# First half of the k weights on ScalarE's DMA queue in two loads, x tile 3 between the row blocks of the second half

## Chip, cores, metric

The kernel runs on one core of a Trainium2 chip. The metric is the device time of one execution in microseconds; the time before is the median of three runs.

## What is computed

The input x has 2048 rows of 640. It is layer-normalised; from the normalised rows come q, k and v, and a linear attention with 32 heads of 20 columns; a small expert block works on the eight rows with the largest routing score; both are added to x. Cut to what matters here:

```python
xn = _layernorm(x, axis=-1)
qkv = (xn @ wqkv)                       # wqkv is 640 x 1920: q, k, v columns
phi = lambda t: jnp.where(t > 0, t + 1, jnp.exp(t)) + 1e-6
pq, pk = phi(q), phi(k)
kv = jnp.einsum("bhsd,bhse->bhde", pk, v)
o = num / den                           # from pq, kv and the sum of pk
r = xn @ w_r                            # routing score, one number per row
return x + o @ wo + expert_update(xn, top 8 of r)
```

## The kernel before

**Tiles.** x is held as 16 tiles of 128 rows in `XX[:, t, 1, :]` (raw) and `XX[:, t, 0, :]` (normalised). `wkh[0]` holds columns 0 to 319 of the k weights, all five row blocks of 128 (128 partitions x 5 x 320 bf16, 400 KB); `wkh[1]` holds columns 320 to 639, and a 321st column with w_r, which lets the k matmul of the second half give the routing score too. w_r is loaded as five rows (`wr`), transposed by TensorE (L136) and copied into that column by ScalarE (L139).

**Order.** The schedule is written by hand: the instructions of each engine run in the order of the code, and each DMA queue (SyncE's, `sp`, and ScalarE's, `act`) in the order of its issues. There are eight landing semaphores, used in turn, so a load can also wait until the load issued eight before it has landed.

**The front.** The loads of the first microseconds are x tiles 0, 1, 2 (L105, L111, L112), `wkh[0]` in one load (L113), x tile 3 (L114), the five row blocks of `wkh[1]` (L140 to L141), then x tiles in pairs (L365 on), all on SyncE's queue; `wr` alone is on ScalarE's queue (L110). Meanwhile VectorE works on the layer norm of each tile: statistics of the two halves (`ln_a`, L157, and `ln_b`, L160), their aggregate (`ln_g`, L163), variance plus epsilon (L188), the power -0.5 on GpSimd (L190), the centred copy `c` (`ln_c`, L197), the reciprocal (L202) and the scaled result (`ln_xn`, L204). The statistics of tile 1 are made on ScalarE (`ln_act`, L171 to L175) and turned to a variance on VectorE (`ln_var`, L182). VectorE's written order of the front is

```python
ln_a(0); ln_b(0); ln_g(0); ln_s(0); ln_c(0, dve)
ln_a(2)                                  # needs x tile 2
ln_xn(0, ...)                            # behind ln_a(2) on VectorE
ln_var(1); ln_s(1, -1.0); ln_c(1, dve); ln_b(2); ln_xn(1)
ln_g(2); ln_s(2); ln_c(2, dve)
ln_a(3)                                  # needs x tile 3
ln_xn(2)
```

The first four normalised tiles are transposed by TensorE (`tr_pe`, L211) and copied out by ScalarE (L215); `K(t)` (L242) is the k matmul of a tile, five row blocks for each half of the columns; `PHe` and `PHr` (L258, L261) are exponential and relu on ScalarE, `PHb` (L277) is min-and-add on VectorE, and `G(t)` (L282, L287) multiplies the normalised tile with the result and accumulates over all tiles. From tile 4 on one loop runs over the tiles; the q matmuls (L493), the small products and the output matmuls (L744) follow.

Of the kernel before, what the change touches and what calls it, by code (L numbers as in the profile page):

```python
# [9 lines left out]
D = 640  # L10
# [28 lines left out]
def kernel(  # L39
# [13 lines left out]
    pe, dve, act, pool, sp = nc.tensor, nc.vector, nc.scalar, nc.gpsimd, nc.sync  # L53

    x_v = A_x[0].rearrange("(t p) d -> p t d", p=P)
    out_v = out[0].rearrange("(t p) d -> p t d", p=P)
    wqkv_v = A_wqkv.rearrange("(kc p) n -> p kc n", p=P)
# [9 lines left out]
    def st(shape, dt, name, tag=None):  # L67
        return sb.tile(shape, dt, name=name, tag=tag or name)

    XX = st([P, T, 2, D], BF16, "XX")  # L70
# [26 lines left out]
    HW = 320  # L97
    wkh = [wk[:, 0 : KC * HW].rearrange("p (k c) -> p k c", k=KC),
           wk[:, KC * HW : KC * (D + 1)].rearrange("p (k c) -> p k c", k=KC)]


    def ld(eng, dst, src):
        eng.dma_start(dst, src)
# [4 lines left out]
    dve.memset(MVf[:], 0.0)  # L108
    wr = st([KC, P], BF16, "wr")
    ld(act, wr[:], B_w_r.rearrange("(kc p) -> kc p", p=P))  # L110
    ld(sp, XX[:, 1, 1, :], x_v[:, 1, :])  # L111
    ld(sp, XX[:, 2, 1, :], x_v[:, 2, :])  # L112
    ld(sp, wkh[0], wqkv_v[:, :, D : D + HW])  # L113
    ld(sp, XX[:, 3, 1, :], x_v[:, 3, :])  # L114


    zero32 = zero[:].bitcast(F32)
# [20 lines left out]
    warm(1)  # L138
    act.copy(wkh[1][:, :, HW], PS[:, 3, :].bitcast(BF16)[:, 0:KC])  # L139
    for kc in range(KC):  # L140
        ld(sp, wkh[1][:, kc, 0:HW], wqkv_v[:, kc, D + HW : 2 * D])  # L141
    kv1 = st([P, NG, GC], BF16, "kv1")
    kv2 = st([P, NG, GC], BF16, "kv2")
# [793 lines left out]
```

## Time and profile before

| | us |
|---|---|
| median of 3 runs | 109.39 |
| lowest, highest | 108.97, 109.47 |
| the profiled execution | 108.93 |
| its span, first to last instruction | 107.2 |

| engine | busy us | share of the span |
|---|---|---|
| PE (matmul) | 101.2 | 94% |
| PEld (weight load) | 62.3 | 58% |
| DVE | 85.0 | 79% |
| ACT | 74.8 | 70% |
| POOL | 25.5 | 24% |

The granted TensorE clock is full in the whole span. In lines of the trace SPq and ACTq are the queues' issuing instructions, not work of the engine; a timeline line gives start, duration, engine, line, operation, tiles, shapes and count, and in brackets the idle time before it with what ended it. A line of a load gives its size and the time from issue to landing. The loads are made in a helper, so all of them have line L103; they are told apart by tile and time.

### The profile page before, as it was taken

What the parts mean: (1) busy time and instruction counts of PE and PEld (TensorE: products, weight loads), DVE (VectorE), ACT (ScalarE), POOL (GpSimd) and SP (SyncE); (2) the same over time, 40 slices, a digit from 0 to 9 for tenths busy, and PEclk for the clock granted to TensorE, in tenths of its full rate; (3) what the DMA queues carried; (4) which work ended last, traced back from release to release, by engine and by line L of the source; (5) the groups of instructions that cost most, each with busy time, mean ns of one, the idle gap of its engine ahead of it and who ended that gap; (6) DMA issues with size and microseconds to landing.
All of it is one profiled execution on the core that took longest, in us unless ns stands there. A gap on an engine that the chain in (4) does not pass through costs nothing.

```text
span 107.2 us, 2572 instructions
## 1 busy us (share of the span) xinstructions
PE 101.2 (94%) x908; PEld 62.3 (58%) x918; DVE 85.0 (79%) x210; ACT 74.8 (70%) x163; POOL 25.5 (24%) x72
## 2 busy tenths in 40 slices
PE   5979999999999999999999999999999999999970
PEld 1246656666666666666556555655656677777740
DVE  1899999979999999974888987539599696798860
ACT  4649996887887777888696999988687699100000
POOL 7326216346222222000000583400008000000410
PEclk9999999999999999999999999999999999999999
DMA  2998991523565765899998999911550243895342
GB/s 77 262 318 258 323 148 38 104 43 73 122 141 122 118 135 120 184 236 369 274 401 271 317 339 383 296 35 43 205 173 0 63 147 101 207 369 200 124 134 74
DMA packets 23135, 19.68 MB, mean 184 GB/s; under 512 B 10578, under 2 KB 21586, under 8 KB 23122
## 3 DMA queue, kind: packets, MB, share of 16 engines
q1 hardware_dynamic: 22600, 19.41, 63.1%
q8 instruction: 7, 0.11, 0.4%
q10 hardware_dynamic: 234, 0.09, 0.3%
q0 software_dynamic: 288, 0.01, 0.3%
q14 instruction: 6, 0.05, 0.1%
HBM read 13.80 MB, written 3.65 MB: 163 GB/s over the span
## 4 chain that ended last, share of the span: by engine, by line
PE 82%; DVE 9%; DMA 2%; POOL 2%; issue 1%
PE PS L493 20%; PE PS L744 20%; PE PS L242 15%; PE PS L282 15%; PE PS L287 4%; DVE XX L204 2%; DMA XX<-in_A_x_dram 2%; POOL s L190 2%; PE PS L669 2%; PE PS L706 2%; DVE pk L277 1%; DVE stats L157 1%; DVE stats L160 1%; PE PS L557 1%; PE PS L728 1%
## 5 line engine op out<-in xcount | busy, mean ns | idle before, releaser
L242 PE MATMUL PS<-wk,xnT 128*128 128x320 bf16 (+1 forms) x160 | 24.6, 300 | 0.6 <-DMA wk<-in_A_wqkv_dram 0.6
L493 PE MATMUL PS<-xnT,wq 128*128 128x512 bf16 x95 | 22.7, 380 | 0.3
L282 PE MATMUL PS<-pk,XX 128*128 128x512 bf16 x75 | 22.3, 379 | 0.2 <-DVE pk L277 0.2
L744 PE MATMUL PS<-Mb,pqT 128*128 128x320 bf16 x160 | 22.1, 299 | 0.0
L242 PEld LDWEIGHTS <-xnT 128*128 128x128 bf16 x160 | 15.5, 98 | 7.3 <-ACT xnT L215 0.6
L744 PEld LDWEIGHTS <-pqT 128*128 128x128 bf16 x160 | 15.5, 97 | 6.5 <-issue 0.2
L258 ACT ACTIVATE ek<-PS 128x320 bf16<-128x320 f32 x32 | 14.2, 444 | 5.0 <-PE PS L242 5.0
L493 PEld LDWEIGHTS <-wq 128*128 128x128 bf16 x100 | 11.3, 118 | 9.0
L190 POOL TENSOR_TENSOR s<-t,halfc 128x1 bf16<-128x1 bf16 x16 | 9.9, 617 | 25.5 <-DVE t L188 25.5
L548 DVE SCALAR_TENSOR_TENSOR pqT<-qe,qr 128x512 bf16<-128x512 bf16 x20 | 13.5, 685 | 2.0 <-ACT qr L500 1.7
L758 DVE TENSOR_TENSOR o<-PS,XX 128x640 bf16<-128x640 f32 x15 | 12.2, 821 | 3.5 <-PE PS L744 3.2
L499 ACT ACTIVATE qe<-PS 128x512 bf16<-128x512 f32 x20 | 12.2, 609 | 3.8 <-PE PS L493 3.3
L261 ACT ACTIVATE rk<-PS 128x320 bf16<-128x320 f32 x32 | 14.3, 447 | 0.0
L287 PE MATMUL PS<-pk,XX 128*128 128x128 bf16 x64 | 14.0, 219 | 0.3
L277 DVE SCALAR_TENSOR_TENSOR pk<-ek,rk 128x640 bf16<-128x640 bf16 x16 | 13.0, 815 | 0.8 <-ACT rk L261 0.7
L282 PEld LDWEIGHTS <-XX 128*128 128x128 bf16 x80 | 7.7, 98 | 8.1
L500 ACT ACTIVATE qr<-PS 128x512 bf16<-128x512 f32 x20 | 12.1, 605 | 0.0
L195 ACT ACTIVATE c<-XX,MVf 128x640 bf16<-128x640 bf16 x10 | 8.4, 836 | 2.1 <-DVE MVf L163 1.4
L232 ACT ACTIVATE XX<-XX,MR,SR 128x640 bf16<-128x640 bf16 x11 | 9.4, 914 | 0.0
L157 DVE BATCH_NORM_STATS2 stats<-XX 128x6 f32<-128x320 bf16 x14 | 6.8, 487 | 1.9 <-DMA XX<-in_A_x_dram 1.9
L204 DVE TENSOR_SCALAR XX<-c,SR 128x640 bf16<-128x640 bf16 (+2 forms) x17 | 6.5, 389 | 1.7 <-ACT rk L261 0.5
L583 DVE TENSOR_TENSOR pqT<-pqT,R 128x1280 bf16<-128x1280 bf16 x8 | 6.5, 818 | 0.6 <-DMA R<-rd_d 0.6
(121 smaller groups left out, 101.6 us busy)
## 6 DMA issues: line engine op xcount, KB each, us to landing
out_dram<-o SPq DMA_DIRECT2D x15, 160.0 KB, 2.3
XX<-in_A_x_dram SPq DMA_DIRECT2D x6, 320.0 KB, 6.0
wg<-in_B_w_gate_dram SPq DMA_DIRECT2D x5, 384.0 KB, 7.7
wu<-in_B_w_up_dram SPq DMA_DIRECT2D x5, 384.0 KB, 6.1
wd<-in_B_w_down_dram SPq DMA_DIRECT2D x1, 1920.0 KB, 11.1
wv<-in_A_wqkv_dram SPq DMA_DIRECT2D x5, 160.0 KB, 2.9
wq<-in_A_wqkv_dram SPq DMA_DIRECT2D x1, 800.0 KB, 5.0
hi_d<-XX SPq DMA_DIRECT2D x1, 800.0 KB, 4.6
```

The lines of the kernel that those rows point to most:

```text
L242: pe.matmul(PS[:, b + h, off(t, h) : off(t, h) + w], lhsT=xnT[:, kc, t * P : (t + 1) * P], rhs=wkh[h][:, kc, 0:w], start=(kc == 0), stop=( ...
L258: act.activation(phis[t][0][:, h * HW : (h + 1) * HW], phi_src(t, h, b), AF.Exp)
L261: act.activation(phis[t][1][:, h * HW : (h + 1) * HW], phi_src(t, h, b), AF.Relu)
L277: dve.scalar_tensor_tensor(out=pk[:, t, :], in0=ek[:], scalar=1.0, in1=rk[:], op0=ALU.min, op1=ALU.add)
L282: pe.matmul(PS[:, a, :], lhsT=lhsT, rhs=pk[:, t, 0:512], start=(t == 0), stop=(t == T - 1),)
L287: pe.matmul(PS[:, 5, a * P : (a + 1) * P], lhsT=lhsT, rhs=pk[:, t, 512:D], start=(t == 0 and a == 0), stop=(t == T - 1), skip_group_check= ...
L493: pe.matmul(PS[:, bank, :], lhsT=by5(wq[:, kc, :])[:, m, :], rhs=xnT[:, kc, tb * TBLK : (tb + 1) * TBLK], start=(kc == 0), stop=(kc == KC ...
L499: act.activation(e, PS[:, bank, :], AF.Exp)
L500: act.activation(r, PS[:, bank, :], AF.Relu)
L548: dve.scalar_tensor_tensor(out=pqT[:, m, tb * TBLK : (tb + 1) * TBLK], in0=e, scalar=1.0, in1=r, op0=ALU.min, op1=ALU.add,)
L744: pe.matmul(PS[:, b + h, 0:HW], lhsT=pqT[:, kc, t * P : (t + 1) * P], rhs=Mb[:, kc, h * HW : (h + 1) * HW], start=(kc == 0), stop=(kc == K ...
L758: dve.tensor_tensor(out=ot[:].rearrange("p (h c) -> p h c", h=2), in0=PS[:, b : b + 2, 0:HW], in1=XX[:, t, 1, :].rearrange("p (h c) -> p h ...
```

## The change

`wkh[0]` is taken from SyncE's queue and issued from ScalarE's, right behind `wr`, as two loads: row blocks 0 and 1 (160 KB), and row blocks 2 to 4 (240 KB). The load of x tile 3 moves behind row blocks 0 and 1 of `wkh[1]` on SyncE's queue. No arithmetic changes, and each compute engine's instructions keep their order.

```diff
     ld(act, wr[:], B_w_r.rearrange("(kc p) -> kc p", p=P))
+    for a, b in ((0, 2), (2, 5)):
+        ld(act, wkh[0][:, a:b, :], wqkv_v[:, a:b, D : D + HW])
     ld(sp, XX[:, 1, 1, :], x_v[:, 1, :])
     ld(sp, XX[:, 2, 1, :], x_v[:, 2, :])
-    ld(sp, wkh[0], wqkv_v[:, :, D : D + HW])
-    ld(sp, XX[:, 3, 1, :], x_v[:, 3, :])
...
     for kc in range(KC):
+        if kc == 2:
+            ld(sp, XX[:, 3, 1, :], x_v[:, 3, :])
         ld(sp, wkh[1][:, kc, 0:HW], wqkv_v[:, kc, D + HW : 2 * D])
```

## The prediction

> **What bounds the kernel now.** I read the page first (span, shares), then the chain that ended last in order of time, then the waits and sums of each engine before and after the point where the chain changes engine, and last the loads of the first ten microseconds one by one.
>
> The page and the chain:
> ```profile
> span 107.2 us, 2572 instructions
> PE 82%; DVE 9%; DMA 2%; POOL 2%; issue 1%
> ...
> 0.79 2.27 DMA XX<-in_A_x_dram
> ...
> 4.40 0.29 DVE c L197
> 4.70 0.02 issue
> 4.71 0.49 DVE stats L157
> 5.21 0.13 DVE SR L202
> ...
> 14.27 0.74 DVE pk L277
> 15.01 0.04 issue
> 15.05 0.38 PE PS L282
> ```
> The chain has two parts. From the landing of x tile 0 (0.79 + 2.27 = 3.06 us) to 15.01 it is VectorE's layer norm of the first tiles, with the power on GpSimd in between. From 15.05 on it is TensorE. The busy times of the two stretches (PE, PEld, DVE, ACT, POOL, then clock, DMA share and GB/s) and the waits inside them:
> ```profile
> 3.05:15.05 12.00, 11.10 (x73) 6.30 (x74) 11.38 (x38) 9.88 (x31) 4.18 (x12) 1.00 1.01 271
> 15.05:105.00 89.95, 88.24 (x834) 55.53 (x842) 73.31 (x170) 63.66 (x132) 18.91 (x49) 1.00 0.62 178
> ...
> DVE stats L157 <- DMA XX<-in_A_x_dram: 1.9, 1, 1.9
> ...
> PE PS L282 <- DVE pk L277: 0.2, 1, 0.2
> ```
> VectorE is busy 11.38 of 12.00 us in the first stretch, and its one listed wait is that for x tile 0. After 15.05 TensorE has one wait, 0.2 us in 90. So the front costs its length: a microsecond that VectorE loses before 15.05 moves the end by a microsecond, and one that another engine gains there is worth nothing unless VectorE was waiting for it. At full speed (clock 1.00) the rest has no room to give anything back. The profiled execution took 108.93 us, 1.73 more than its span; the median of the three runs is 109.39, so I add changes to 109.39. About 0.5% (0.55 us) is what a measurement here can tell from no change.
>
> **What is removed, added, moved.** The issues of the front in SyncE's and ScalarE's queue, and the one stall of the former:
> ```profile
> 0.79 1.35 SPq L103 DMA_DIRECT2D XX<-in_A_x_dram  x3
> 0.82 0.57 ACTq L103 DMA_DIRECT2D wr<-in_B_w_r_dram  x1
> 2.19 0.43 SPq L103 DMA_DIRECT2D wk<-in_A_wqkv_dram  x1
> 2.66 0.53 SPq L103 DMA_DIRECT2D XX<-in_A_x_dram  x1
> 3.23 2.34 SPq L103 DMA_DIRECT2D wk<-in_A_wqkv_dram  x5
> 5.61 3.59 SPq L103 DMA_DIRECT2D XX<-in_A_x_dram  x6
> ...
> SPq L103 <- DMA wk<-in_A_wqkv_dram: 0.7, 1, 0.7
> ```
> Three x loads in 1.35 us are 0.45 each: tiles 0, 1, 2 go out at 0.79, 1.24, 1.69. The first half of the k weights follows at 2.19, x tile 3 at 2.66, the five row blocks of the second half from 3.23, the pairs of x tiles from 5.61.
>
> *The first half, now on ScalarE's queue.* It follows the load of w_r, which ends at 0.82 + 0.57 = 1.39. At 0.43 to 0.57 each the two loads are issued at about 1.4 and 1.9 and done by 2.3 to 2.5: the first (160 KB, row blocks 0 and 1) about when x tile 2 is issued, the second (240 KB) after it. ScalarE has nothing to do until its copy at 3.46, so the issuing itself costs nothing:
> ```profile
> 3.46 0.18 ACT L139 COPY wk<-PS 128x5 bf16<-128x5 bf16 x1 [1.39 <-PE PS L136]
> 3.53 0.74 ACT L171 ACTIVATE junk<-XX 128x640 bf16<-128x640 bf16 x1
> ...
> 5.12 0.19 ACT L175 ACTIVATION_READ_ACCUMULATOR junk<-XX 128x1 f32 x1
> ...
> 5.79 0.22 DVE L182 SCALAR_TENSOR_TENSOR MVf<-sm 128x1 bf16<-128x1 f32 x1
> ```
> *What the earlier weights give.* The first k matmul waited for them:
> ```profile
> 6.65 0.66 PEld L242 LDWEIGHTS <-xnT 128*128 128x128 bf16 x5 [0.60 <-ACT xnT L215]
> 6.80 0.84 PE L242 MATMUL PS<-wk,xnT 128*128 128x320 bf16 x5 [0.58 <-DMA wk<-in_A_wqkv_dram]
> ...
> 9.28 0.48 ACT L261 ACTIVATE rk<-PS 128x320 bf16<-128x320 f32 x1
> ...
> 10.40 0.82 DVE L277 SCALAR_TENSOR_TENSOR pk<-ek,rk 128x640 bf16<-128x640 bf16 x1
> ```
> The 0.58 looks like the prize and is not: the transposed tile reached TensorE at 6.65, so the weights were late by 0.15 alone. What hangs on it is ScalarE's exponentials and VectorE's first min-and-add at 10.40, whose input was done at 9.76, 0.64 earlier. On the chain this is worth 0; if that 0.64 of cover were gone it would be worth at most 0.15.
>
> *What they cost.* The 400 KB now compete with x tiles 1 and 2. Landing times of single loads (tile 1, tile 2, tile 3, and row blocks 0 and 4 of the second half; last column, us from issue) and the traffic while tiles 1 and 2 arrive:
> ```profile
> XX<-in_A_x_dram SPq DMA_DIRECT2D x1, 160.0 KB, 2.3
> ...
> XX<-in_A_x_dram SPq DMA_DIRECT2D x1, 160.0 KB, 3.0
> ...
> XX<-in_A_x_dram SPq DMA_DIRECT2D x1, 160.0 KB, 4.5
> ...
> wk<-in_A_wqkv_dram SPq DMA_DIRECT2D x1, 80.0 KB, 4.2
> ...
> wk<-in_A_wqkv_dram SPq DMA_DIRECT2D x1, 80.0 KB, 3.3
> ...
> 2.40:3.00 0.60, 0.60 (x2) 0.00 (x0) 0.00 (x0) 0.00 (x0) 0.60 (x3) 1.00 1.00 341
> 3.00:4.00 1.00, 1.00 (x3) 0.60 (x3) 0.89 (x2) 0.54 (x2) 0.09 (x1) 1.00 0.79 173
> ```
> Tile 2 lands at 1.69 + 3.0 = 4.7, and VectorE's statistics of tile 2 start at 4.71, right behind c of tile 0: no slack at all, and the statistics stand ahead of tile 0's own scaling in VectorE's order, so everything behind waits with them. 160 KB put ahead of tile 2 take 164 KB / 341 GB/s = 0.48 us. Upper end: tile 2 lands at 4.7 + 0.48 = 5.18, VectorE loses 0.47. Lower end: tile 2 had 3.0 where tiles 0 and 1 had 2.3; with 2.3 it would land at 4.0, with the 0.48 at 4.47, still in time: 0. A gain is excluded here, since VectorE could not start before 4.70 anyway. From 3.0 to 4.0 the DMA engines were 0.79 busy, so some 0.2 of the 0.48 falls into idle time; that leaves 0.28, and I take +0.3. Tile 1 is read by ScalarE at 3.53; ScalarE is done with it at 5.31 and VectorE asks at 5.79, so it may be 0.4 late for nothing. Tile 0's last rows could meet the first weight rows: 0 to +0.1, taken as 0, as its data are nearly all in by then.
>
> Is it right to put the weights ahead by order of issue? The one small load from ScalarE's queue while SyncE's was full says so:
> ```profile
> krow<-c ACTq DMA_DIRECT2D x1, 0.5 KB, 4.2
> ```
> Half a kilobyte took 4.2 us where 160 KB on empty engines took 2.3: it did not pass what was issued before it. The Trainium skill, "DMA: Bandwidth & Descriptors", section "Queues, rings and completion order", has each DMA engine take turns between the queues, a packet at a time; by that the ScalarE load would have got its turn early, which this row does not show. By the rule x tile 2 would still wait for one packet of weights on each engine, about the same 160 KB, and the sum would not change much. The section "Issuing engines are not separate DMA queues" of the same page speaks against the change: a second queue saves issue time and no transfer time.
>
> *SyncE's queue.* With the first half gone, row block 0 is issued at 2.19. Row block 1 has to wait for ScalarE's copy (its columns span those that the copy writes), which ends at 3.64; so SyncE idles about a microsecond and issues it at 3.7, as now (3.23 + 0.47). x tile 3 follows at 4.2 instead of 2.66, row blocks 2 to 4 at 4.7, 5.1, 5.6, the first pair at 6.1 instead of 5.61. The 0.7 stall behind the pair goes, because the weights it waits for have long landed, so the later pairs are out some 0.2 earlier: worth 0, no VectorE wait names them. Row block 4 is issued 0.47 later, with fewer bytes queued ahead: about the same landing.
>
> Tile 3 is wanted at 8.04:
> ```profile
> 8.04 0.49 DVE L157 BATCH_NORM_STATS2 stats<-XX 128x6 f32<-128x320 bf16 x1
> ```
> With 2.3 it lands at 6.5, with the 3.3 to 4.2 of the row blocks around it at 7.5 to 8.4, with its own 4.5 of now at 8.7. Its 4.5 came from standing behind the 400 KB that now are ahead by two microseconds, so I take 3.3, 7.5: cost 0, cover 0.5 us.
>
> Sum: 0 (weights earlier) + 0.3 (tile 2) + 0 (tile 3, pairs) = +0.3, with 0 and +0.5 as its ends: 109.39 + 0.3 = 109.7, within the half per cent.
>
> **Rivals.** (a) *Both loads ahead of tile 2: slower.* If ScalarE's second load is served before tile 2 as well (ScalarE issues quicker than 0.57, or SyncE's issues stretch while both queues issue), 400 KB stand ahead: 410 KB / 341 GB/s = 1.20 us. Tile 2 lands at 5.2 (from 4.0) to 5.9 (from 4.7), and VectorE loses 0.5 to 1.2: 109.9 to 110.6. For it: tile 2's landing is already 0.7 worse than tile 1's with nothing beside it. Against: the second load's issue ends after tile 2's. It decides from a landing at 5.26 on.
>
> (b) *Tile 3 late: slower.* If its load keeps 4.5 it lands at 8.7, 0.66 after VectorE wants it. It decides where tile 2 was in time; else VectorE comes later too and the two overlap. 110.0 to 110.1. Against: fewer bytes ahead.
>
> (c) *Faster.* The profiled execution is 0.46 below the median. If the usual run loses that in the front to weights that land past the 0.64 of cover, the change gives it back: 109.39 - 0.46 = 108.9, and with the 0.15 of the first matmul 108.8. Against: nothing in this profile shows VectorE waiting for weights.
>
> (d) *It does nothing:* tile 2 lands early enough, the weights were never on the chain: 109.4. This is the lower end of the forecast.
>
> **How the numbers follow.** Forecast with (d), 109.4 to 109.9: 0.52. (a) 0.28, (b) 0.10, (c) 0.10. Faster by over 0.5% (below 108.84) is (c): 0.10; slower by over 0.5% (above 109.94) is (a) and (b): 0.38; between them 0.52. The range goes up into (a) to 110.4, leaving out about a quarter of it, 0.07, and down to 109.0, which leaves out most of (c), 0.08: 109.0 to 110.4.
>
> **What would show it.** In the profile after: tile 2's landing (4.5 to 5.2 expected), and VectorE's second L157-type statistics starting as much later than 4.71; a DMA wait for x on VectorE beside the first; the first k matmul at or before its transposed tile, with no weight wait; SyncE's gap before row block 1; tile 3 landed by about 7.5; TensorE's unbroken part starting at 15.05 plus what VectorE lost, and as long as now. Wrong would be: VectorE reaching 15.0 earlier, a new TensorE wait after 15.05, or tile 3 as the late one.

## The result: slower by 0.7%

| | before | changed |
|---|---|---|
| median of 17 runs each, us | 109.27 | 109.98 |
| lowest, us | 108.85 | 109.46 |
| the profiled execution, us (span) | 108.93 (107.2) | 109.96 (108.2) |

The ratio is 1.0074, 95% interval 1.005 to 1.0098. The ratios here and below leave out executions more than 1.5% above the fastest of their kernel (2 of 17 before, 3 of 17 changed; 3 of 12 in e9 and e10, 2 of 6 in e1 and e4, else one or none), while the medians do not; over all executions the means of the two kernels differ by the same 0.74%. Lines from L141 on have moved down by two in the changed kernel (L157 is now L159, L242 is L244), in the experiments by up to five.

Three lines of the profile before, to compare with: the k matmuls of tile 0's second half with those behind them, VectorE's min-and-adds at the end of the front, and TensorE behind them.
```profile
7.87 1.58 PE L242 MATMUL PS<-wk,xnT 128*128 128x321 bf16 x10
...
14.18 1.55 DVE L277 SCALAR_TENSOR_TENSOR pk<-ek,rk 128x640 bf16<-128x640 bf16 x2
...
15.05 0.38 PE L282 MATMUL PS<-pk,XX 128*128 128x512 bf16 x1 [0.15 <-DVE pk L277]
```
VectorE's front in the profile after:
```profile
3.16 0.49 DVE L159 BATCH_NORM_STATS2 stats<-XX 128x6 f32<-128x320 bf16 x1 [1.93 <-DMA XX<-in_A_x_dram]
...
5.02 0.49 DVE L159 BATCH_NORM_STATS2 stats<-XX 128x6 f32<-128x320 bf16 x1 [0.24 <-DMA XX<-in_A_x_dram]
...
14.53 1.55 DVE L279 SCALAR_TENSOR_TENSOR pk<-ek,rk 128x640 bf16<-128x640 bf16 x2
```
x tile 0 is 0.08 us later than before, and there is the new wait for x tile 2, 0.24 us. At 14.53 VectorE is 0.35 late (14.18 before). TensorE in the same profile:
```profile
7.06 0.85 PE L244 MATMUL PS<-wk,xnT 128*128 128x320 bf16 x5 [0.37 <-ACT xnT L217]
...
9.61 0.97 PE L244 MATMUL PS<-wk,xnT 128*128 128x321 bf16 x6 [0.77 <-DMA wk<-in_A_wqkv_dram]
...
14.35 1.53 PE L244 MATMUL PS<-wk,xnT 128*128 128x320 bf16 x10
15.72 0.38 PE L284 MATMUL PS<-pk,XX 128*128 128x512 bf16 x1
```
The wait for the first half of the weights is gone, as intended. But the last k matmul of tile 0's second half waits 0.77 us for row block 4, and TensorE comes out 0.67 late at the matmul that stood at 15.05. That is more than VectorE's 0.35: VectorE's first min-and-add of the two at 14.53 was done at about 15.35 (it takes 0.82), and TensorE was still busy with k matmuls until 15.72. The chain that ended last runs through that load:
```profile
1.71 3.29 DMA XX<-in_A_x_dram
5.00 0.02 issue
5.01 0.40 SPq L103
5.42 0.04 issue
5.46 4.11 DMA wk<-in_A_wqkv_dram
9.57 0.04 issue
9.61 0.97 PE PS L244 x6
...
14.92 0.70 ACT junk L173 x2
...
24.66 0.74 DVE pk L279
25.40 0.04 issue
25.44 0.38 PE PS L284
```
Read from the top: x tile 2 lands at 5.00; SyncE issues row block 3 right behind it, at 5.01, because the two loads share one of the eight landing semaphores; row block 4 follows at 5.46 and lands at 9.57. The semaphores are not taken strictly eight loads apart: row block 3 is the sixth load issued after tile 2, but in the trace its issue waits on tile 2's semaphore. In this execution that held it back by some 0.03 us only, since SyncE was done with the load before at 4.94. What made row block 4 late is its own 4.11 us from issue to landing, 3.3 before.

ScalarE, a microsecond late after it, does tile 5's statistics later, and through VectorE that stops TensorE once more, at 25.44. Before, the chain stayed on TensorE from 15.05 on. The span is 1.0 longer: 0.67 from the front, and the remaining 0.3 from two short stops, 0.13 at 22.50 and 0.16 at 25.44 (the starts of the same matmuls in the two traces compared).

SyncE's own waits were as worked out: the 0.7 us stall is gone, and a gap in front of row block 1 has come.
```profile
SPq L103 <- ACT wk L139: 1.0, 1, 1.0
```

### The profile page after: what moved, and what is told of

It is laid out like the page before. It is cut to its first block, busy times and chain, and to the rows that moved or that the text cites. A ratio compares the mean times of both kernels' runs of the same rounds, so it can differ in the third digit from the quotient of the medians.

```text
span 108.2 us, 2573 instructions
## 1 busy us (share of the span) xinstructions
PE 101.6 (94%) x908; PEld 62.5 (58%) x918; DVE 85.1 (79%) x210; ACT 74.8 (69%) x163; POOL 25.4 (23%) x72
## 4 chain that ended last, share of the span: by engine, by line
PE 74%; DMA 7%; ACT 6%; DVE 5%; POOL 2%; issue 1%; SPq 1%; ACTq 1%; DVEq 0%
PE PS L495 20%; PE PS L746 20%; PE PS L244 12%; PE PS L284 11%; DMA wk<-in_A_wqkv_dram 4%; DMA XX<-in_A_x_dram 3%; PE PS L289 3%; ACT ek L260 2%; POOL s L192 2%; PE PS L671 2%; PE PS L708 2%; ACT rk L263 1%; SPq L103 1%; PE PS L559 1%; DVE XX L206 1%
## 5 line engine op out<-in xcount | busy, mean ns | idle before, releaser
L244 PE MATMUL PS<-wk,xnT 128*128 128x320 bf16 (+1 forms) x160 | 24.7, 300 | 1.1 <-DMA wk<-in_A_wqkv_dram 0.8
L244 PEld LDWEIGHTS <-xnT 128*128 128x128 bf16 x160 | 15.4, 98 | 8.1 <-ACT xnT L217 1.6
L159 DVE BATCH_NORM_STATS2 stats<-XX 128x6 f32<-128x320 bf16 x14 | 6.8, 486 | 2.2 <-DMA XX<-in_A_x_dram 2.2
```

Source lines behind the costliest of these rows:

```text
L244: pe.matmul(PS[:, b + h, off(t, h) : off(t, h) + w], lhsT=xnT[:, kc, t * P : (t + 1) * P], rhs=wkh[h][:, kc, 0:w], start=(kc == 0), stop=( ...
```

## The experiments

Ratios are to the kernel before, in runs on the same chip. The edits of e1, e3 and e4 are shown against the changed kernel, that of e2 against the kernel before, and of e5 the added lines alone. Landing times that stand in no line shown are from the traces' records of landings. Two theories stood at the start. A: row block 4 is issued too late. B: ScalarE's loads share the DMA engines with x tiles 0 to 2, and what follows on VectorE is late.

**e1, ScalarE's loads alone.**
```diff
     ld(sp, XX[:, 2, 1, :], x_v[:, 2, :])
+    ld(sp, XX[:, 3, 1, :], x_v[:, 3, :])
...
-        if kc == 2:
-            ld(sp, XX[:, 3, 1, :], x_v[:, 3, :])
```


> One half of the change alone: the first half of the k weights comes from ScalarE's queue in two loads as in the changed kernel, but x tile 3 goes ahead of the row blocks of the second half on SyncE's queue (into the slot that the first half left), so row blocks 2 to 4 are issued about 0.45 us earlier than in the changed kernel. Theory A (the changed kernel loses its time because row block 4 of the second half lands late, 9.57 against 8.43 us, and TensorE waits for it): block 4 lands near 9.0 or before, TensorE's wait of 0.77 us shrinks to 0.3 or less, and the time comes back by about half, 109.5 to 109.7. Theory B (the time is lost on VectorE by x tiles 0 and 2 landing later): tile 2 still lands near 5.0 and the time stays where the changed kernel is, ratio about 1.007 to before.

Measured: ratio 1.0124 (1.007 to 1.0179), slower than the whole change if anything. VectorE's and TensorE's timeline, and SyncE's queue waits:
```profile
6.11 0.49 DVE L158 BATCH_NORM_STATS2 stats<-XX 128x6 f32<-128x320 bf16 x1 [1.29 <-DMA XX<-in_A_x_dram]
...
9.99 1.95 PE L243 MATMUL PS<-wk,xnT 128*128 128x321 bf16 x10
...
SPq L103 <- DMA XX<-in_A_x_dram: 1.6, 1, 1.6
```
Tile 2 landed at about 6.1, and VectorE stood 1.29 us for it. SyncE was held 1.6 us by tile 2's landing, so row blocks 3 and 4 were issued later than in the changed kernel (6.10 and 6.47) instead of earlier. Row block 4 landed at 8.70 even so, 0.87 earlier, and TensorE did not wait for it; yet the time did not come back. Tile 2's landing therefore delays two things, VectorE and the issue of the last two row blocks, and in this run the second cost nothing that shows.

**e2, the move of x tile 3 alone.**
```diff
     ld(sp, wkh[0], wqkv_v[:, :, D : D + HW])
-    ld(sp, XX[:, 3, 1, :], x_v[:, 3, :])
...
+        if kc == 2:
+            ld(sp, XX[:, 3, 1, :], x_v[:, 3, :])
```


> The other half of the change alone: the first half of the k weights stays in one load on SyncE's queue, and x tile 3 goes behind row blocks 0 and 1 of the second half. Row blocks 2 to 4 are issued as late as in the changed kernel (4.6 to 5.5 us), x tile 2 has no second queue beside it. Theory A: block 4 lands at 9 us or later, TensorE waits for it, ratio 1.003 to 1.008 to before. Theory B: tile 2 lands at 4.7 or before, VectorE loses nothing, ratio 1.000.

Measured: ratio 1.0009 (0.9981 to 1.0037): no change that can be told. The profiled execution was one of its slowest (110.31) and shows TensorE's wait:
```profile
9.75 0.97 PE L243 MATMUL PS<-wk,xnT 128*128 128x321 bf16 x6 [0.99 <-DMA wk<-in_A_wqkv_dram]
```
Row block 4 landed at 9.71 there, as theory A had it, and tile 2 at 4.92, with VectorE waiting 0.21 for it, where theory B had 4.7 and nothing. So single executions with a late row block and a slightly late tile 2 exist without ScalarE's loads, but the later issue alone costs nothing in the mean that can be told. Theory A as the whole cause is out; the 0.7% come with ScalarE's loads.

**e3, x tile 1 at the head of ScalarE's queue, so tile 2 is issued 0.45 us earlier.**
```diff
+    ld(act, XX[:, 1, 1, :], x_v[:, 1, :])
     ld(act, wr[:], B_w_r.rearrange("(kc p) -> kc p", p=P))
...
-    ld(sp, XX[:, 1, 1, :], x_v[:, 1, :])
```


> The changed kernel with x tile 1 taken to the head of ScalarE's queue, so that x tile 2 is issued 0.45 us earlier on SyncE's and should land at 4.5 or before; row block 4 is issued as late as in the changed kernel. Theory A: VectorE's wait for tile 2 (0.24 us) goes, TensorE still waits for block 4, time as the changed kernel, ratio 1.005 to 1.008 to before. Theory B: the time comes back by 0.3 us or more, ratio 1.004 or less.

Measured: ratio 1.0143 (1.0109 to 1.0177), worse than the change, which neither theory expected. VectorE's timeline, and the landings of tiles 0 and 1 (last column, us from issue):
```profile
3.76 0.50 DVE L159 BATCH_NORM_STATS2 stats<-XX 128x6 f32<-128x320 bf16 x1 [2.52 <-DMA XX<-in_A_x_dram]
...
XX<-in_A_x_dram SPq DMA_DIRECT2D x1, 160.0 KB, 2.9
XX<-in_A_x_dram ACTq DMA_DIRECT2D x1, 160.0 KB, 3.1
```
Tiles 0 and 1, issued almost together from two queues, took 2.9 and 3.1 us where each took 2.3 one behind the other. Tile 0 started VectorE 0.68 late. Tile 2 landed at 4.40 as planned, and VectorE did not wait for it, but as a test of tile 2 the run fell through, since it hurt tile 0 (and w_r). It shows that loads of two queues share the DMA engines and delay each other.

**e4, the second half of the weights without SyncE's wait for the copy.**
```diff
-    act.copy(wkh[1][:, :, HW], PS[:, 3, :].bitcast(BF16)[:, 0:KC])
+    act.copy(wrc[:], PS[:, 3, :].bitcast(BF16)[:, 0:KC])
...
+    for kc in range(KC):
+        pool.tensor_copy(wkh[1][:, kc, HW : HW + 1], wrc[:, kc : kc + 1])
...
-    for kc in range(KC):
-        if kc == 2:
+    for a, b in ((0, 2), (2, 5)):
+        if a:
             ld(sp, XX[:, 3, 1, :], x_v[:, 3, :])
-        ld(sp, wkh[1][:, kc, 0:HW], wqkv_v[:, kc, D + HW : 2 * D])
+        ld(sp, wkh[1][:, a:b, 0:HW], wqkv_v[:, a:b, D + HW : 2 * D])
```


> The changed kernel without SyncE's wait for ScalarE's copy of the w_r column: the second half is laid out with a padded row, the copy goes to a small tile, and GpSimd puts the five columns in place afterwards; the second half is loaded in two loads (row blocks 0 and 1, then 2 to 4) with x tile 3 between, all issued by 3.6 us. x tile 2 is as in the changed kernel. Theory A: the second half lands by 7.5, TensorE does not wait for it, and only VectorE's 0.3 us are left: 109.5, ratio 1.003 or less to before. Theory B: as the changed kernel, ratio 1.007.

Measured: ratio 1.0395 (1.0344 to 1.0446). The edit made a wait of its own:
```profile
POOL wk L156 <- DMA wk<-in_A_wqkv_dram: 5.3, 2, 4.5
```
GpSimd's five copies waited for the loads beside which they write, 4.5 us the first time, and the powers of the layer norm stood behind them. In its profile VectorE also waited 1.75 us for tile 2. It does not tell A from B.

**e5 and e6, ScalarE's loads held back.** Two small GpSimd memsets in the destination, behind its large ones, hold both loads until 2.75 us; the loads and the copy move down in the code accordingly.
```diff
     pool.memset(kv2[:], 0.0)
+    for a in (0, 2):
+        pool.memset(wkh[0][:, a, 0:2], 0.0)
     pool.memset(xsT[:], 0.0)
     pool.tensor_copy(identf[:], ident[:])
+    for a, b in ((0, 2), (2, 5)):
+        ld(act, wkh[0][:, a:b, :], wqkv_v[:, a:b, D : D + HW])
```
e5 is the changed kernel with the hold; e6 is e1 with it.

> The changed kernel with ScalarE's two loads held back by about 1.3 us, to 2.7 and 3.2 us (two small GpSimd memsets in their destination, after its large memsets, release them), so that x tiles 0 to 2 have the DMA engines to themselves. SyncE's queue is as in the changed kernel, row block 4 of the second half is issued at 5.5. Theory B (the change costs time because ScalarE's loads share the DMA engines with x tiles 0 to 2, so that tile 2's last share lands late on VectorE): tile 2 lands at 4.8 or before, and the time is that of the kernel with the x tile 3 move alone, ratio 1.000 to 1.003 to before. Theory A (row block 4, or another effect of the second queue later on): ratio 1.006 to 1.009, as the changed kernel.

> The same hold in the kernel with x tile 3 ahead of the second half's row blocks (ScalarE's loads alone moved; 1.0124 without the hold, tile 2 landed at 6.1 and SyncE's queue stood 1.6 us behind it). Theory B: tile 2 lands at 4.8 or before, SyncE does not wait for it, ratio 1.003 or less. If the loss comes from x tile 3 and row block 0 being issued earlier on SyncE's own queue: tile 2 still lands at 5.5 or later, ratio 1.008 or more.

Measured: e5 1.0012 (0.9985 to 1.0038), e6 1.0014 (0.9985 to 1.0043). Both intervals stay below those of the same kernels without the hold (from 1.005 and from 1.007 up). ScalarE's queue, VectorE and TensorE in e5:
```profile
2.75 0.92 ACTq L103 DMA_DIRECT2D wk<-in_A_wqkv_dram  x2
...
4.68 0.49 DVE L161 BATCH_NORM_STATS2 stats<-XX 128x6 f32<-128x320 bf16 x1
...
6.72 0.85 PE L246 MATMUL PS<-wk,xnT 128*128 128x320 bf16 x5 [0.43 <-ACT xnT L219]
...
8.92 1.19 PE L246 MATMUL PS<-wk,xnT 128*128 128x321 bf16 x7 [0.40 <-DMA wk<-in_A_wqkv_dram]
```
Tile 2 is in time at 4.68, with no idle time before it (it landed at 4.18); the weights, issued 1.3 us later than in the changed kernel, still keep no matmul of the first half waiting. TensorE still waits 0.40 in the second half, now for row block 3, which landed at 8.87 (seven matmuls follow, its own, that of row block 4 and five of tile 1), and that costs little. In e6's profile tile 2 landed at 4.91 and VectorE waited 0.19 for it, where it waited 1.29 without the hold; SyncE waited 0.2, where it waited 1.6. Theory B had expected 4.8 and no wait of SyncE there, so it was missed by a little in the profile and held in the time. Theory B holds: what costs is that the loads run beside x tiles 0 to 2, not that they come from ScalarE.

**e7 and e8, both kernels once more,** one execution each.

> The kernel before once more, for a second look at its front: tile 2 lands at 4.6 to 5.0, VectorE waits 0 to 0.3 us for it, and row block 4 of the second half lands between 8.2 and 8.8, with no wait of TensorE for it.

> The changed kernel once more. Theory B: tile 2 lands at 5.0 or later and VectorE waits 0.2 us or more for it. Theory A: row block 4 lands at 9.3 or later and TensorE waits 0.5 us or more.

VectorE at tile 2, first the kernel before (110.17 us), then the changed one (111.64 us), with TensorE's first k matmuls in the latter:
```profile
5.07 0.49 DVE L157 BATCH_NORM_STATS2 stats<-XX 128x6 f32<-128x320 bf16 x1 [0.29 <-DMA XX<-in_A_x_dram]
```
```profile
5.67 0.50 DVE L159 BATCH_NORM_STATS2 stats<-XX 128x6 f32<-128x320 bf16 x1 [0.86 <-DMA XX<-in_A_x_dram]
...
6.64 0.71 PE L213 MATMUL PS<-ident,XX 128*128 128x128 bf16 x5 [0.78 <-DVE XX L206]
7.72 1.51 PE L244 MATMUL PS<-wk,xnT 128*128 128x320 bf16 x5 [0.36 <-ACT xnT L217]
...
9.56 1.88 PE L244 MATMUL PS<-wk,xnT 128*128 128x321 bf16 x10
```
Tile 2's landing varies between executions of one kernel: VectorE waited 0 and 0.29 before, 0.24 and 0.86 after. Two executions each would not tell the kernels apart, but the profiles together point one way: tile 2 landed between 4.18 and 5.04 in the six without ScalarE's loads beside it (before twice, e2, e5, e6, e10), and at 5.00, 5.65 and 6.08 in the changed kernel's two and e1. The expectation for the kernel before that TensorE does not wait for row block 4 missed: it landed at 9.16, and TensorE waited 0.31. In e8 theory A's sign did not come: row block 4, issued at 6.04 because SyncE was held by tile 2, landed at 8.23, and TensorE did not wait for it.

**e9, the second of ScalarE's loads alone held back.** The memset for row block 2 and the load of blocks 2 to 4 stay as in e5; blocks 0 and 1 go back behind w_r.

> The changed kernel with ScalarE's first load (row blocks 0 and 1) as in it, at 1.4 us, and the second (row blocks 2 to 4) alone held back to 2.7 us. It splits the loss found between the two loads. If 160 KB ahead of x tile 2 are what delays it (the step of the prediction): tile 2 lands at 5.0 or later, ratio 1.005 or more to before. If the 240 KB of the second load, which share the DMA engines with tile 2's last rows, are what does it: tile 2 lands at 4.8 or before, ratio 1.003 or less.

Measured: ratio 1.0037 (1.001 to 1.0063), between the two outcomes expected. VectorE waited for tile 2, which landed at 4.87, also between the two; TensorE waited 0.7 for row blocks 3 and 4:
```profile
4.90 0.50 DVE L160 BATCH_NORM_STATS2 stats<-XX 128x6 f32<-128x320 bf16 x1 [0.25 <-DMA XX<-in_A_x_dram]
```
None held 1.0074, the second held 1.0037, both held 1.0012: by these values each load takes a share. The intervals of neighbours in this row overlap and only the ends are apart, so how the loss divides between the two loads is not shown.

**e10, a try at a better version:** e5 with x tile 3 between row blocks 0 and 1 (`if kc == 1`).

> A try at a version better than both: both ScalarE loads held, and x tile 3 between row blocks 0 and 1 of the second half, in the time in which SyncE waits for ScalarE's copy anyway. Against the hold alone row blocks 2 to 4 are issued about 0.45 us earlier, and little stands right behind x tile 2. Tile 2 at 4.2 to 4.8, row block 4 by 8.6, no TensorE wait for it: ratio 0.997 to 1.001 to before. If the hold's tie with the kernel before is not set by row block 4, it stays at 1.001.

Measured: ratio 1.0011 (0.9985 to 1.0036). Its profile has no wait of VectorE beyond tile 0 and no listed wait of a k matmul for weights; tile 2 landed at 4.54 and row block 4 at 8.16, and the profiled execution took 108.93 us. No version was found that beats the kernel before.

## Why the prediction came out as it did

The measured 109.98 lies in the range, and 0.3 above the 109.7 forecast. The change itself was more than twice as large as forecast: +0.7 us between the medians (the kernel before has 109.27 here, where the prediction added to 109.39) and +0.8 by the ratio, where +0.3 stood. The direction and the place, the landing of x tile 2, were right. The case held likeliest, within half a per cent, was missed by a little: 0.74%, with the interval from 0.5% on. That the range held the result is owed to its upper part, which was there for rival (a).

- *Weights earlier, worth 0*: right. The first k matmul waits for the transposed tile only, and e5, with the weights 1.3 us later, is no slower.
- *Tile 2 late, +0.3 (0 to 0.47)*: right in place and kind, and shown by the hold. VectorE's wait was 0.24 in the profiled execution, 0.86 in e8 and 1.29 in e1, so the upper bound was too low. One reason is its starting point: I took the profile's 4.7 as the latest landing without ScalarE's loads, and e7 and e2 had 5.04 and 4.92.
- *Order of issue*: wrong. The krow load's 4.2 us was read as one queue not passing the other. e3 shows two queues sharing from the start (2.9 and 3.1 us against 2.3). That is what the Trainium skill says in "DMA: Bandwidth & Descriptors", section "Queues, rings and completion order": each DMA engine takes turns between queues. So 160 KB was not a safe count of what tile 2 meets, and the second load may count too, as e9's value hints. The measured +0.7 to +0.8 lies inside rival (a)'s 0.5 to 1.2, but its sign, a landing from 5.26 on, came in e8 (5.65) and not in the profiled execution (5.00).
- *A microsecond of VectorE moves the end by a microsecond, and other engines count only where VectorE waits*: the step that was mis-sized. VectorE began tile 2 later by 0.31 us in the profiled execution, and TensorE left the front 0.67 later; in e8 by 0.96 and 1.53, in e1 by 1.40 and 2.03. In the profiled execution the rest is TensorE's wait of 0.77 for row block 4; in e8 and e1 it is TensorE itself, which ran its first k matmuls at half pace (last section). Neither had a term in the sum.
- *Row block 4, about the same landing*: not so in the profiled execution, 9.57 against 8.43. Its issue at 5.46 was earlier than the 5.6 worked out; the landing took longer. Its landing does not follow its issue: 5.14 gave 8.43 and, in e7, 9.16; 5.46 gave 9.57 and, without ScalarE's loads in e2, 9.71; 6.04 in e8 gave 8.23. I had also followed each load by its issue and its bytes and not by its landing semaphore: row block 3 cannot go before tile 2 has landed (1.6 us of standing in e1). No run shows that this cost time. What makes row block 4 late in some executions, and whether the change makes it later in the mean, stays open.
- *Tile 3*: right, it landed at 6.93 in the profile after, with no wait for it anywhere. *SyncE's gap and the lost stall*: right, 1.0 and gone. *Rival (b)* and *(c)*: not seen.

## What to carry to other kernels

Before moving a load to a second queue, look which transfers are on their way at that moment and whether the first consumer has slack: here a load that nobody waited for took DMA time from one that VectorE was waiting for. If the second queue is wanted, hold its loads until the urgent ones are through; the hold cost nothing here that can be told (1.0012, 0.9985 to 1.0038) and took the loss away. And when loads share a small set of landing semaphores, a late landing also holds back the issue of the load that takes that semaphore next (0.7 us in e8, 1.6 in e1, without a loss that shows), so follow the turns as well as the bytes.

## What was not expected of the hardware

- A tile's landing is set by its last share. A load of this size is told as landed by 16 completions, and the last ones can lag: of tile 2's, 13 had come by 4.83 us in e1 and the last at 6.08; in e8 15 by 4.78 and the last at 5.65. Always issued at 1.7 us, tile 2 landed at 4.18 (e5), 4.69 and 5.04 (before), 5.00 and 5.65 (changed) and 6.08 (e1). The early loads of ScalarE's queue move it up; what else decides in a single execution is not shown.
- In e8 the first five k matmuls took 1.51 us where they took 0.85 in the profile after, while the page's granted clock was at or near full in both. The page prints full also where the trace has no clock record, so "full in the whole span", said of the kernel before, holds from the first record on. That is at 5.25 us before, at 6.55 in the profile after, and at 10.27 in e8, 10.83 in e1 and 9.45 in e3. Until then the k matmuls of these three started 0.27 us apart, behind it 0.14. In e8 TensorE fell back by 1.1 us in this way, from 0.92 late at its first k matmul to 2.03 at its ninth. The Trainium skill, "TensorE: Matmul & The Clock Gate", section "Part 1: The HAM clock gate (the "warmup" mystery)", says that a TensorE that has not been busy runs at half rate; these traces agree, 0.27 against 0.14 us. In these three TensorE began tile 0's transposes at 6.42 to 7.08; in the others, e4 aside, it began at 6.03 or before, and full speed is recorded from 6.95 or before. So by these traces a late tile can also cost TensorE its speed for some microseconds.
